# Mixing K and V of three of four batches by 64x64 matrices in four tiles of the array, with a new order of all units

## The chip, the cores and the metric

The kernel runs on one core of one Trainium2 chip. The metric is the device time of one execution in microseconds; a stated time is the median of several executions. Beside it stands one execution that was taken by the hardware profiler, from which all views below come. Its engines are named as the profile names them: PE multiplies matrices and PEld loads their weights, DVE and ACT do vector and activation work and empty PSUM, POOL is the fourth engine and also issues the casting loads, SP issues most other transfers.

## What is computed

```python
P = sort_net                                    # (4, 8, 8, 8): batch, head, 8x8
for _ in range(5):
    P = exp(P - max(P, -1)); P = P / sum(P, -1); P = P / sum(P, -2)
k_sorted = einsum('bhij,bhjcd->bhicd', P, k_b)  # blocks of 96 tokens, D = 64
v_sorted = einsum('bhij,bhjcd->bhicd', P, v_b)
attn = softmax(q_b @ k_sorted_b^T / sqrt(D))    # each block with itself
x = attn @ v_sorted_b                           # (4, 768, 512) over all heads
h = relu(x @ w_in)                              # 512 -> 1024, halves u and v
v_n = layernorm(v)                              # over 512 features
v_s = w_spatial @ v_n + b_spatial               # 768 x 768 over tokens
out = (u * v_s) @ w_out                         # 512 -> 512
```

There are 4 batches, 8 heads (4 pairs of heads), 768 tokens in 8 blocks of 96, and 64 features per head.

## The kernel before

The program is a list of units. The string `ORDER` names them one after the other, with their PSUM place, the engine that empties it, the batch and the head pair or tile; every engine runs what the units give it in that order, and nothing reorders it afterwards. `KT:1:A:2:0`, for example, mixes K of batch 2, head pair 0, into PSUM pair 1, and ACT empties it. PSUM is 8 banks; a place under 10 is a pair of banks, 10 to 17 a single bank.

The units and their lines: `L` loads a tensor over POOL's queue, casting to bf16, into one of eight slots (`ld`); `LH` brings half of batch 0's Q over SP's queue. `SK` is one round of the iteration on P. `MA`, `MB`, `MC` make masks and spreading matrices from the identity (L221 to L227), `PR` spreads P over the partitions by matmuls, and `P0` (on DVE, batch 0) and `PD` (on POOL, later batches) multiply it with a mask into `pd`: for each head a 128x128 matrix. A load puts 6 consecutive tokens of a head into each of 128 partitions, so a 128x128 matrix that is P[i,j] times an identity of 16 mixes the blocks without any movement of tokens.

`QT` turns Q by PE transposes, `QP` and `QX` by a copy and a transposing DMA (batches 2 and 3). `KT` mixes and turns K in one step: 12 matmuls with K as the weights (L395), the two heads of a pair in the two halves of the array's columns; `natural` copies the result to SBUF in token order. `VT` and `VB` do the same for V of batch 0 and turn it back. For batches 1 to 3 `VM` mixes V (L422: two matmuls of 128x128 weights and 384 columns per head pair) into the single buffer `vm`, and `VC` (L435) copies it by SP's DMAs, one per block, into `vb`, in which a block's 96 tokens lie in the partitions. `SC` computes a half of a head pair's scores (L454) and their exponent (L459); `AT` multiplies by `vb` (L500), and DVE divides by the sum (L507, L508).

Behind it comes the second part: `XT` or `XD` turn the attention's output, `VP` and `VH` compute the v half of the first layer (L567), `ST`, `LN` and `LA` its normalisation, `UP` the u half (L613), `SP` the spatial product (L625), `GT` the gating, `OP`, `OE` and `OS` the last layer and its output (L651). `SH`, `GH`, `OH`, `OI` and `OJ` do the last batch in smaller pieces. `WT` and `WW` turn the spatial weights.

Before the tail, `CK` gathers whether the sums of the softmax and of P left a safe range; `CF` (L747 to L749) adds it up into `flag`, `LF` (L752) loads it into a register of every engine, and `IF` branches to the tail or to a slower general path.

## Time and profile before

| | us |
|---|---|
| time, median of 3 runs (149.43 to 153.02) | 151.65 |
| span of the profiled execution | 147.7 |
| PE busy in it | 141.4 (96%) |
| PEld (weight loads, beside PE) | 101.0 (68%) |
| DVE busy | 115.1 (78%) |
| ACT busy | 85.2 (58%) |
| POOL busy | 39.1 (26%) |

The page gives no time of the profiled execution beside its span. Busy shares are averages over the whole span, in which different stages have different limits. The tables by windows of time tell the stages apart, and the chain of waits in order of time lists the work that each next piece waited for.

### The profile page before, as it was taken

Reading aid. Unit: us, or ns where it says so; the run is one execution under the profiler, and the core shown is the slowest. Engines: PE = TensorE matmul, PEld = TensorE weight load, DVE = VectorE, ACT = ScalarE, POOL = GpSimd, SP = SyncE. Lnnn points to the kernel's source line nnn. Section 1 sums busy time; section 2 is a strip of 40 time slices with the busy share of each in tenths; the row PEclk is TensorE's granted clock in tenths of the full one; section 3 lists DMA queues with packets and bytes.
Section 4 is the critical chain, followed back from the end, with each engine's and each line's share of the span. In section 5 each row is a group of like instructions: output and inputs, shape, how many; then the busy total and the mean of one; then the engine's idle time right before and its main releaser. Section 6 shows DMA issues by size and latency. Waiting matters only on the chain.

```text
span 147.7 us, 4114 instructions
## 1 busy us (share of the span) xinstructions
PE 141.4 (96%) x1691; PEld 101.0 (68%) x1691; DVE 115.1 (78%) x263; ACT 85.2 (58%) x125; POOL 39.1 (26%) x44
## 2 busy tenths in 40 slices
PE   6997999999999999999999999999999999999991
PEld 2466777857776667776877678768866876854760
DVE  3878899979987978867869879899558989846741
ACT  5357998988789447658793328756640046160040
POOL 6701994410000006991002640000002100004630
PEclk9999999999999999999999999999999999999999
DMA  2999999999999999899999999503602507007856
GB/s 60 278 204 205 204 207 201 208 225 243 227 233 231 204 200 269 131 177 211 206 202 175 213 239 278 132 0 83 28 0 60 190 2 284 0 2 266 307 210 228
DMA packets 37013, 25.93 MB, mean 176 GB/s; under 512 B 16704, under 2 KB 34112, under 8 KB 36992
## 3 DMA queue, kind: packets, MB, share of 16 engines
q0 software_dynamic: 14432, 12.19, 51.9%
q1 hardware_dynamic: 21552, 11.88, 33.8%
q10 hardware_dynamic: 1008, 1.57, 2.8%
q8 instruction: 14, 0.23, 0.6%
q14 instruction: 7, 0.06, 0.1%
HBM read 24.78 MB, written 6.29 MB: 210 GB/s over the span
## 4 chain that ended last, share of the span: by engine, by line
PE 82%; DMA 8%; DVE 5%; POOL 2%; issue 1%; ACT 1%; POOLq 0%; DVEq 0%
PE ps L625 16%; PE ps L567 15%; PE ps L613 14%; PE ps L651 11%; DMA k_in<-in_k_dram 8%; PE ps L681 5%; PE ps L500 4%; PE ps L395 4%; PE ps L701 4%; PE ps L454 4%; PE ps L422 3%; DVE x_sb L508 2%; PE ps L326 1%; PE ps L536 1%; PE ps L530 1%; DVE vb L124 1%
## 5 line engine op out<-in xcount | busy, mean ns | idle before, releaser
L642 POOL TENSOR_TENSOR gt<-z,u_sb 128x768 bf16<-128x768 f32 x7 | 11.4, 1642 | 68.0 <-DVE z L631 54.7
L459 ACT ACTIVATE ex_all<-ps 96x768 bf16<-96x768 f32 x32 | 23.7, 805 | 5.0 <-PE ps L454 4.1
L625 PE MATMUL ps<-wspT,v_sb 128*128 128x384 bf16 x144 | 25.0, 326 | 0.0
L567 PE MATMUL ps<-w_in_sb,xT 128*128 128x256 bf16 (+1 forms) x176 | 23.8, 283 | 0.0
L613 PE MATMUL ps<-xT,w_in_sb 128*128 128x384 bf16 x128 | 23.0, 326 | 0.0
L128 ACT ACTIVATE u_sb<-ps 128x768 bf16<-128x768 f32 x16 | 13.0, 811 | 17.3 <-PE ps L613 17.2
L508 DVE TENSOR_TENSOR x_sb<-ps,rec_all 96x512 bf16<-96x512 f32 x32 | 22.0, 687 | 1.1
L625 PEld LDWEIGHTS <-v_sb 128*128 128x128 bf16 x144 | 13.5, 98 | 8.4
L567 PEld LDWEIGHTS <-xT 128*128 128x128 bf16 x176 | 16.2, 98 | 4.0
L651 PE MATMUL ps<-w_out_sb,gt 128*128 128x256 bf16 x144 | 16.9, 273 | 0.0
L613 PEld LDWEIGHTS <-w_in_sb 128*128 128x128 bf16 x128 | 12.0, 98 | 7.0
L587 DVE BATCH_NORM_STATS2 stats<-v_sb 128x6 f32<-128x512 bf16 x24 | 16.2, 675 | 0.6 <-ACT v_sb L128 0.5
L122 ACT COPY o_sb<-ps 128x1024 f32<-128x1024 f32 (+2 forms) x11 | 8.9, 830 | 12.6 <-PE ps L701 9.3
L631 DVE TENSOR_TENSOR z<-ps,b_bc 128x768 f32<-128x768 f32 x12 | 11.5, 954 | 5.9 <-PE ps L625 5.1
L651 PEld LDWEIGHTS <-gt 128*128 128x128 bf16 x144 | 13.8, 98 | 2.0
L500 PEld LDWEIGHTS <-ex_all 96*128 96x128 bf16 x256 | 11.1, 97 | 2.6
L500 PE MATMUL ps<-vb,ex_all 96*128 96x65 bf16 x256 | 12.4, 193 | 0.1
L122 ACT CAST vm<-ps 128x768 bf16<-128x768 f32 x9 | 6.8, 807 | 9.7 <-PE ps L422 6.6
L694 POOL TENSOR_TENSOR gt<-z,u_sb 128x512 bf16<-128x512 f32 (+1 forms) x5 | 5.2, 1046 | 21.5 <-DVE z L687 21.5
L507 DVE RECIPROCAL rec_all<-ps 96x8 f32<-96x8 f32 x32 | 6.3, 196 | 5.5 <-PE ps L500 5.3
L130 DVE TENSOR_SCALAR v_sb<-ps 128x512 bf16<-128x512 f32 (+1 forms) x12 | 8.7, 727 | 1.7 <-PE ps L567 1.5
L236 PE MATMUL ps<-warm 128*128 128x512 bf16 (+3 forms) x38 | 8.5, 386 | 1.3 <-DVE warm L210 1.3
(100 smaller groups left out, 199.9 us busy)
## 6 DMA issues: line engine op xcount, KB each, us to landing
v_in<-in_v_dram POOLq DMA_DIRECT2D x4, 768.0 KB, 16.0
k_in<-in_k_dram POOLq DMA_DIRECT2D x4, 768.0 KB, 14.9
vb<-vm SPq DMA_DIRECT2D x24, 99.0 KB, 4.8
q_in<-in_q_dram POOLq DMA_DIRECT2D x3, 768.0 KB, 11.6
out_dram<-o_sb SPq DMA_DIRECT2D x9, 256.0 KB, 2.3
out_dram<-o_sb SPq DMA_DIRECT2D x4, 512.0 KB, 5.9
out_dram<-o_sb ACTq DMA_DIRECT2D x5, 256.0 KB, 2.3
ws_in<-in_moe_w_spatial_dram POOLq DMA_DIRECT2D x2, 576.0 KB, 18.9
```

The costliest lines, as they stand in the source:

```text
L122: nc.scalar.copy(out=out, in_=in_)
L128: nc.scalar.activation(out=out, in_=in_, func=AF.Relu)
L459: nc.scalar.activation(out=e_tile(b, hp, ih).rearrange("p h (x g) -> p h x g", g=G), in_=t[0:BLK, :, 0:HW].rearrange("p h (g x) -> p h x g ...
L500: nc.tensor.matmul(t[:, hh, ii * VW:ii * VW + D + 1], lhsT=e[:, c:c + 128], rhs=vb[b % 2][:, ih * NI + ii, 2 * hp + hh, 0:D + 1], start=Tr ...
L508: nc.vector.tensor_mul(out=x_sb[:, hp].rearrange("p i (h d) -> p h i d", h=2), in0=tv[:, :, :, 0:D], in1=_raw_ap(rec, 0, [rec.ap[0], [NI, ...
L567: nc.tensor.matmul(t[:, x, c:c + DH // parts], lhsT=st["xT", b][:, n // 3, kc, (n % 3) * 128:(n % 3 + 1) * 128], rhs=w_in_sb[:, kc, DH + c ...
L587: nc.vector.bn_stats(out=stats, in_=st["v_sb", b, n])
L613: nc.tensor.matmul(t[:, x, 0:HW], lhsT=w_in_sb[:, kc, mc * 128:(mc + 1) * 128], rhs=st["xT", b][:, ih, kc, :], start=(kc == 0), stop=(kc = ...
L625: nc.tensor.matmul(t[:, x, 0:HW], lhsT=st["v_sb", b, n][:, mc * 128:(mc + 1) * 128], rhs=wspT[:, 3 * x:3 * x + 3, n, :], start=(n == 0), s ...
L631: nc.vector.tensor_add(out=z.rearrange("p (x c) -> p x c", x=2), in0=t[:, :, 0:HW], in1=b_bc.rearrange("p (x c) -> p x c", x=2),)
L642: eng.tensor_mul(out=gt, in0=st["z", b, mc], in1=u)
L651: nc.tensor.matmul(t[:, x, c:c + w], lhsT=st["gt", b, mc][:, (n0 + x) * 128:(n0 + x + 1) * 128], rhs=w_out_sb[:, mc, c:c + w], start=(mc = ...
```

## The change

K and V of batches 1 to 3 are loaded with 12 consecutive tokens per partition and two heads of a pair in the two halves of the 128 partitions, 64 rows each (source runs of 3 KB, not 1.5). `pd` of these batches is one 64x64 matrix per head. `KP` takes the place of `KT` there: it mixes K of two head pairs by 48 matmuls of 64x64 weights and 64 columns, in turn for the four tiles of the array, into two PSUM pairs. `VM` mixes V by four matmuls of 64x64 weights and 384 columns in the four tiles. `VC` issues two DMAs per block, 48 partitions each. The heads of an odd pair change halves (`half`), so `QP` copies them in two pieces. Batch 0 keeps 128 rows (`mixed0`, `pd0`), with masks and spreading matrices of its own, so `MA`, `MB`, `MC` do each step twice and `PR` has 12 matmuls where it had 4.

The whole `ORDER` is new. K of batch 0 is loaded and mixed before V; V of batch 1 is loaded right behind; its mixing and that of batch 2 stand earlier; `CF` and `LF` stand side by side. Of each version the lines around the flag:

```
-UP:3:A:3:1:1 CF:11 VH:12:A:3:2 VH:13:A:3:1 OS:1:2:0:1 OS:1:2:1:2 LF VH:16:A:3:0 GT:D:2:2 OS:1:0:0:1:A OS:1:0:1:2:A
+OS:0:0:1:2:A OS:1:0:0:1:A OP:1:2:2:2 LA:3:4 LA:3:0 LA:3:1 OE:A:2:4 CF:11 LF SH:17:3:1:0 OE:D:2:2 OS:2:0 SH:16:3:2:0
```

The core of the rest of the diff; the same swap of halves is made in the Q transposes and in the general path:

```diff
@@ -169,7 +175,16 @@
 
 
     def u_L(what, *a):
-        if what in ("q", "k", "v"):
+        if what in ("k", "v") and int(a[0]) > 0:
+            b, lo, hi = (int(x) for x in a)
+            src = {"k": k, "v": v}[what]
+            if (what, b) not in st:
+                st[what, b] = ld_tile(f"{what}_in").rearrange("p h c -> p (h c)").rearrange("p (k c) -> p k c", k=HP)
+            nc.gpsimd.dma_start(
+                out=st[what, b][:, lo:hi],
+                in_=_raw_ap(src, (b * H + 2 * lo) * S * D, [[GR * D, 128], [2 * S * D, hi - lo], [1, GR * D]]),
+            )
+        elif what in ("q", "k", "v"):
             b, lo, hi = (int(x) for x in a)
             src = {"q": q, "k": k, "v": v}[what]
             if (what, b) not in st:
@@ -218,13 +233,16 @@
         make_identity(nc, ident)
 
     def u_MA():
-        nc.vector.reduce_sum(out=m32, in_=ident.rearrange("p (j t) -> p t j", t=TB), axis=AX.X)
+        nc.vector.reduce_sum(out=m32, in_=ident.rearrange("p (j t) -> p t j", t=TR), axis=AX.X)
+        nc.vector.reduce_sum(out=m16, in_=ident.rearrange("p (j t) -> p t j", t=TB), axis=AX.X)
 
     def u_MB():
-        nc.vector.tensor_copy(out=mask16, in_=m32)
+        nc.vector.tensor_copy(out=mask8, in_=m32)
+        nc.vector.tensor_copy(out=mask16, in_=m16)
 
     def u_MC():
-        nc.scalar.copy(out=spread, in_=ident[0:BH, 0:BH].to_broadcast([BH, BH, TB]))
+        nc.scalar.copy(out=spread, in_=ident[0:BH, 0:BH].to_broadcast([BH, BH, TR]))
+        nc.scalar.copy(out=spread16, in_=ident[0:BH, 0:BH].to_broadcast([BH, BH, TB]))
 
     def u_IV(n):
         t = vb[int(n)] if int(n) < 2 else vm
@@ -261,27 +279,38 @@
             nc.vector.transpose(out=p_t, in_=p16)
 
     def u_PR(ps):
-        pr = ps_tile(ps)[:, 0, 0:NB * BH].rearrange("p (i y) -> p i y", i=NB)
-        halves = pr.rearrange("p (k i) y -> p i k y", i=NI)
+        t = ps_tile(ps)[:, 0]
+        pr0 = t[:, 0:NB * H].rearrange("p (i y) -> p i y", i=NB)
+        halves = pr0.rearrange("p (k i) y -> p i k y", i=NI)
         for i in range(NI):
             nc.tensor.matmul(
-                halves[:, i], lhsT=spread[:, i * NB:(i + 1) * NB].rearrange("p j t -> p (j t)"),
-                rhs=p_t[:, 0:2 * BH].rearrange("p (k y) -> p k y", k=2), start=True, stop=True,
+                halves[:, i], lhsT=spread16[:, i * NB:(i + 1) * NB].rearrange("p j t -> p (j t)"),
+                rhs=p_t[:, 0:2 * BH].rearrange("p (k y) -> p k y", k=2)[:, :, 0:H], start=True, stop=True,
             )
-        st["pr"] = pr
+        pr = t[:, NB * H:NB * H + NB * (B - 1) * HP].rearrange("p (i y) -> p i y", i=NB)
+        parts = pr.rearrange("p (k i) y -> p i k y", i=NI)
+        turned_p = p_t.rearrange("p (k y h) -> p h k y", k=2, h=2)
+        for i in range(NI):
+            for hh in range(2):
+                nc.tensor.matmul(
+                    parts[hh * 64:hh * 64 + 64, i],
+                    lhsT=spread[:, i * NB:(i + 1) * NB].rearrange("p j t -> p (j t)"),
+                    rhs=turned_p[:, hh, :, HP:], start=True, stop=True,
+                )
+        st["pr0"], st["pr"] = pr0, pr
 
     def pd(b):
         if ("pd", b) not in st:
-            st["pd", b] = att.tile([128, H, 128], BF16, name="pd", tag="pd", bufs=2)
+            st["pd", b] = att.tile([128, HP, 64], BF16, name="pd", tag="pd", bufs=2)
         return st["pd", b]
 
     def u_P0(lo, hi):
         lo, hi = int(lo), int(hi)
-        n, pr = hi - lo, st["pr"]
+        n, pr = hi - lo, st["pr0"]
         nc.vector.tensor_mul(
-            out=pd(0)[:, lo:hi].rearrange("p h (i t) -> p h i t", t=TB),
+            out=pd0[:, lo:hi].rearrange("p h (i t) -> p h i t", t=TB),
             in0=_raw_ap(mask16, 0, [mask16.ap[0], [0, n], [0, NB], [1, TB]]),
-            in1=_raw_ap(pr, lo, [pr.ap[0], [1, n], [BH, NB], [0, TB]]),
+            in1=_raw_ap(pr, lo, [pr.ap[0], [1, n], [H, NB], [0, TB]]),
         )
 
     def u_PC(eng):
@@ -291,12 +320,14 @@
         b, lo, hi = int(b), int(lo), int(hi)
         n = hi - lo
         nc.gpsimd.tensor_mul(
-            out=pd(b)[:, lo:hi].rearrange("p h (i t) -> p h i t", t=TB),
-            in0=_raw_ap(mask16, 0, [mask16.ap[0], [0, n], [0, NB], [1, TB]]),
-            in1=_raw_ap(prep_sb, b * H + lo, [prep_sb.ap[0], [1, n], [BH, NB], [0, TB]]),
-        )
-
-
+            out=pd(b)[:, lo:hi].rearrange("p h (i t) -> p h i t", t=TR),
+            in0=_raw_ap(mask8, 0, [mask8.ap[0], [0, n], [0, NB], [1, TR]]),
+            in1=_raw_ap(prep_sb, (b - 1) * HP + lo, [prep_sb.ap[0], [1, n], [(B - 1) * HP, NB], [0, TR]]),
+        )
+
+    def half(b, hp, hh):
+        lo = 64 * (hh ^ (hp & 1) if b > 0 else hh)
+        return slice(lo, lo + 64)
 
     def turned(x, b, hp):
         if (x, b, hp) not in st:
@@ -309,11 +340,8 @@
         return st[x, b, hp]
 
     def natural(eng, dst, t):
-        to = dst[:, 0:S].rearrange("p (x g) -> p x g", g=G)
-        of = t[:, 0:S].rearrange("p (g x) -> p x g", g=G)
-        for n, e in enumerate(eng):
-            x = slice(n * 128 // len(eng), (n + 1) * 128 // len(eng))
-            copy(e, to[:, x], of[:, x])
+        to = dst[:, 0:S].rearrange("p (i b t g) -> p i b t g", i=NB, b=2, g=G)
+        copy(eng, to, t[:, :, 0:HW].rearrange("p b (g i t) -> p i b t g", g=G, i=NB))
 
     def q_tile(b):
         if ("qT", b) not in st:
@@ -372,10 +402,12 @@
         if ("qp", b) not in st:
             st["qp", b] = ld_tile("qp").rearrange("p h c -> p (h c)").rearrange(
                 "p (k g h d) -> p k g h d", k=HP, g=G, h=2)
-        copy(
-            eng, st["qp", b][:, hp].rearrange("p g h d -> p h g d"),
-            st["q", b][:, 2 * hp:2 * hp + 2].rearrange("p h (g d) -> p h g d", g=G),
-        )
+        to, of = st["qp", b][:, hp], st["q", b][:, 2 * hp:2 * hp + 2].rearrange("p h (g d) -> p h g d", g=G)
+        if hp % 2 == 0:
+            copy(eng, to.rearrange("p g h d -> p h g d"), of)
+        else:
+            for hh in range(2):
+                copy(eng, to[:, :, 1 - hh], of[:, hh])
 
     def u_QX(b, lo, hi):
         b, lo, hi = int(b), int(lo), int(hi)
@@ -388,22 +420,42 @@
         q_hp = q_tile(b)[rows, hp * S:(hp + 1) * S]
         return q_hp.rearrange("p (g t) -> p g t", g=G)[:, :, i * TB:(i + 1) * TB]
 
-    def mixed(x, name, ps, eng, b, hp):
+    def mixed(x, name, ps, eng, b, m):
+        ts = [ps_tile(n) for n in ps]
+        for n in range(GR):
+            for row in range(2):
+                g = (n + G * row) % GR
+                for o in range(2):
+                    rows = slice(64 * row, 64 * row + 64)
+                    nc.tensor.matmul(
+                        ts[o][half(b, o, row), g // G, (g % G) * 64:(g % G) * 64 + 64],
+                        lhsT=st[x, b][rows, 2 * m + o, g * D:(g + 1) * D], rhs=pd(b)[rows, 2 * m + o, :],
+                        start=True, stop=True,
+                    )
+        for o in range(2):
+            natural(eng[o], turned(name, b, 2 * m + o), ts[o])
+
+    def u_KP(ps0, ps1, eng, b, m):
+        mixed("k", "kT", (ps0, ps1), eng, int(b), int(m))
+
+    def mixed0(x, name, ps, eng, b, hp):
         t = ps_tile(ps).rearrange("p x c -> p (x c)")
         for g in range(G):
             for hh in range(2):
                 nc.tensor.matmul(
                     t[hh * 64:hh * 64 + 64, g * 128:(g + 1) * 128],
-                    lhsT=st[x, b][:, 2 * hp + hh, g * D:(g + 1) * D], rhs=pd(b)[:, 2 * hp + hh, :],
+                    lhsT=st[x, b][:, 2 * hp + hh, g * D:(g + 1) * D], rhs=pd0[:, 2 * hp + hh, :],
                     start=True, stop=True,
                 )
-        natural(eng, turned(name, b, hp), t)
+        copy(
+            eng, turned(name, b, hp)[:, 0:S].rearrange("p (x g) -> p x g", g=G),
+            t[:, 0:S].rearrange("p (g x) -> p x g", g=G))
 
     def u_KT(ps, eng, b, hp):
-        mixed("k", "kT", ps, eng, int(b), int(hp))
+        mixed0("k", "kT", ps, eng, int(b), int(hp))
 
     def u_VT(ps, eng, b, hp):
-        mixed("v", "vT", ps, eng, int(b), int(hp))
+        mixed0("v", "vT", ps, eng, int(b), int(hp))
 
     def u_VB(ps, eng, b, hp):
         b, hp = int(b), int(hp)
@@ -418,11 +470,13 @@
     def u_VM(ps, eng, b, hp):
         b, hp = int(b), int(hp)
         t = ps_tile(ps)
-        for hh in range(2):
-            nc.tensor.matmul(
-                t[:, hh, 0:G * D], lhsT=pd(b)[:, 2 * hp + hh, :], rhs=st["v", b][:, 2 * hp + hh, :],
-                start=True, stop=True,
-            )
+        for gh in range(2):
+            for hh in range(2):
+                rows = slice(64 * hh, 64 * hh + 64)
+                nc.tensor.matmul(
+                    t[64 * gh:64 * gh + 64, hh, 0:G * D], lhsT=pd(b)[rows, hp, :],
+                    rhs=st["v", b][rows, hp, gh * G * D:(gh + 1) * G * D], start=True, stop=True,
+                )
         copy(
             eng,
             vm[:, :, 2 * hp:2 * hp + 2, 0:D].rearrange("p g h d -> p h g d"),
@@ -432,10 +486,12 @@
     def u_VC(b, lo, hi, h0=0, h1=HP, eng="S"):
         b, heads = int(b), slice(2 * int(h0), 2 * int(h1))
         for i in range(int(lo), int(hi)):
-            queue(eng).dma_start(
-                out=vb[b % 2][:, i, heads].rearrange("c h d -> c (h d)"),
-                in_=vm[i * TB:(i + 1) * TB, :, heads].rearrange("t g h d -> t g (h d)"),
-            )
+            for gh in range(2):
+                rows = slice(64 * gh + i * TR, 64 * gh + (i + 1) * TR)
+                queue(eng).dma_start(
+                    out=vb[b % 2][gh * TR * G:(gh + 1) * TR * G, i, heads].rearrange("c h d -> c (h d)"),
+                    in_=vm[rows, :, heads].rearrange("t g h d -> t g (h d)"),
+                )
 
     def e_tile(b, hp, ih):
         e = ex[count["e"] % NE]
@@ -450,7 +506,7 @@
         for ii in range(NI):
             i = ih * NI + ii
             for hh in range(2):
-                rows = slice(hh * 64, hh * 64 + 64)
+                rows = half(b, hp, hh)
                 nc.tensor.matmul(
                     t[:, hh, 0:HW].rearrange("p (g x) -> p g x", g=G)[:, :, ii * TB:(ii + 1) * TB],
                     lhsT=kT[rows, i * BLK:i * BLK + 128], rhs=q_runs(b, hp, rows, i),
```

How the change moves instructions is shown at three places. First, PE around the flag. Before, from the last matmuls ahead of `CF` (L747) to `LF` (L752):

```order
L613 MATMUL ps<-xT,w_in_sb 128x384
L747 LDWEIGHTS ones
L747 MATMUL ps<-bad,ones 1x5 [waits DVE_49]
L567 LDWEIGHTS xT [waits DMAHW5_49]
L567 MATMUL ps<-w_in_sb,xT 128x256 [waits DVE_49]
...
L567 LDWEIGHTS xT
L752 TENSOR_LOAD flag [waits DVE_49]
L567 MATMUL ps<-w_in_sb,xT 128x256 [waits Activation_49]
```

Now:

```order
L707 MATMUL ps<-w_out_sb,gt 128x256
L803 LDWEIGHTS ones
L803 MATMUL ps<-bad,ones 1x5 [waits Activation_49]
L737 LDWEIGHTS v_sb [waits DVE_49]
L808 TENSOR_LOAD flag [waits DVE_49]
L737 MATMUL ps<-wspT,v_sb 128x512
L737 LDWEIGHTS v_sb [waits DVE_49]
```

The load stood behind 16 matmuls of `VH` that follow the flag's own matmul; now only one weight load lies between them.

Second, DVE where it empties batch 2's mixed V into `vm` for the first time. Before (L631 adds the bias to the spatial product, L642 is the gating):

```order
L631 TENSOR_TENSOR z<-ps,b_bc 128x768 [waits PE_49]
L642 TENSOR_TENSOR gt<-z,u_sb 128x768
L631 TENSOR_TENSOR z<-ps,b_bc 128x768 [waits DVE_49,PE_49]
L124 CAST vm<-ps 128x2x6x64 [waits DMAHW4_49,DMAHW3_49,DMAHW5_49,DMAHW2_49,DMAHW6_49,DMAHW1_49,DMAHW7_49,DMAHW0_49,PE_49]
L587 BN_STATS stats<-v_sb 128x6 [waits Activation_49]
L588 BN_AGGR mv<-stats 128x2 [waits DVE_49]
L124 CAST kt_all<-ps 128x768 [waits PE_49] x2
L130 TENSOR_SCALAR v_sb<-ps 128x512 [waits PE_49,Activation_49]
```

Now:

```order
L644 BN_AGGR mv<-stats 128x2 [waits DVE_49]
L563 RECIPROCAL rec_all<-ps 96x8 [waits PE_49]
L564 TENSOR_TENSOR x_sb<-ps,rec_all 96x2x4x64 [waits DVE_49]
L132 TENSOR_SCALAR v_sb<-ps 128x512 [waits PE_49,Activation_49]
L126 CAST vm<-ps 128x2x6x64 [waits DMAHW4_49,DMAHW3_49,DMAHW5_49,DMAHW2_49,DMAHW6_49,DMAHW1_49,DMAHW7_49,DMAHW0_49,PE_49]
L643 BN_STATS stats<-v_sb 128x6
L644 BN_AGGR mv<-stats 128x2 [waits DVE_49]
L563 RECIPROCAL rec_all<-ps 96x8 [waits PE_49]
L564 TENSOR_TENSOR x_sb<-ps,rec_all 96x2x4x64 [waits DVE_49]
```

In both, the copy waits for all eight queues on which the copies from `vm` of batch 1 were sent; before it lies behind the first spatial products, now among the first layer's v half (L132) and the normalisation (L643, L644) of batch 0 and the attention of batch 1.

Third, SP's queue at the end of the copies of batch 1's V into `vb` (L435 before, L491 now). Before:

```order
L435 DMA vb_98<-vm 96x1x528 [waits DMAHW0_49]
L435 DMA vb_98<-vm 96x1x528 [waits DMAHW1_49]
L518 DMA_TRANSPOSE xT<-x_sb 128x16x96 [waits DMAHW2_49,DVE_49]
L382 DMA_TRANSPOSE qT<-qp 128x24x128 [waits DMAHW3_49,PE_49,Activation_49]
L518 DMA_TRANSPOSE xT<-x_sb 128x16x96 [waits DMAHW4_49,DVE_49]
L435 DMA vb_97<-vm 96x1x528 [waits DMAHW5_49,DVE_49,Activation_49]
```

Now:

```order
L491 DMA vb_102<-vm 48x1x528 [waits DMAHW0_49]
L491 DMA vb_102<-vm 48x1x528 [waits DMAHW1_49]
L491 DMA vb_101<-vm 48x1x528 [waits DMAHW2_49,DVE_49,Activation_49]
L491 DMA vb_101<-vm 48x1x528 [waits DMAHW3_49]
L491 DMA vb_101<-vm 48x1x528 [waits DMAHW4_49,PE_49]
```

Before, the eight copies are followed by the transposing DMAs of batch 1's output and batch 2's Q (L518, L382); now sixteen copies stand there, half as many partitions each, and batch 2's copies, which wait for DVE and ACT to have filled `vm` again, follow them directly.

More of the change, by code (lines that the diff above doesn't have):

```diff
@@ L88 @@
     TB = 128 // NB
+    GR = 2 * G
+    TR = 64 // NB
     BH = B * H
@@ L134 @@
     p_t = const.tile([BH, NB * NB], BF16, name="p_t")
-    spread = const.tile([BH, BH, TB], BF16, name="spread")
+    spread = const.tile([BH, BH, TR], BF16, name="spread")
+    spread16 = const.tile([BH, BH, TB], BF16, name="spread16")
     rowsum = const.tile([BH, NB], FP32, name="rowsum")
@@ L471, in u_SM @@
             for hh in range(2):
-                rows = slice(hh * 64, hh * 64 + 64)
+                rows = half(b, hp, hh)
                 nc.tensor.matmul(
```

115 lines of the change are left out of this document (64 added, 51 removed).

## The prediction

> **What bounds the kernel now.** I read the page first: how long the span is and which engine fills it.
>
> ```profile
> span 147.7 us, 4114 instructions
> PE 141.4 (96%) x1691; PEld 101.0 (68%) x1691; DVE 115.1 (78%) x263; ACT 85.2 (58%) x125; POOL 39.1 (26%) x44
> PE 82%; DMA 8%; DVE 5%; POOL 2%; issue 1%; ACT 1%; POOLq 0%; DVEq 0%
> ```
>
> PE is busy 96% of the span and holds 82% of the chain that ended last. An average does not say where, so the second view is the windows of 4 us (busy us of each engine in each).
>
> ```profile
> 12.00:16.00 4.00, 3.36 (x84) 2.78 (x83) 3.42 (x7) 3.14 (x5) 1.91 (x2) 1.00 1.32 206
> 16.00:20.00 4.00, 3.88 (x103) 3.18 (x98) 3.85 (x6) 3.91 (x7) 4.00 (x6) 1.00 1.31 202
> 20.00:24.00 4.00, 3.79 (x95) 3.12 (x94) 3.90 (x10) 3.58 (x6) 2.72 (x4) 1.00 1.32 205
> 24.00:28.00 4.00, 3.86 (x74) 2.92 (x72) 3.82 (x9) 4.00 (x6) 0.89 (x1) 1.00 1.30 208
> 28.00:32.00 4.00, 4.00 (x103) 3.17 (x98) 3.10 (x6) 3.58 (x6) 1.99 (x2) 1.00 1.18 210
> 140.00:144.00 4.00, 4.00 (x29) 2.45 (x28) 1.96 (x5) 1.76 (x3) 1.41 (x2) 1.00 0.51 197
> ```
>
> The columns are PE, PEld, DVE, ACT, POOL and the granted clock. From 28 us to the tail PE is full at clock 1.00. Before that DVE is as full as PE: 14.99 of the 16 us from 12 to 28. So there are two stages: up to 28 us a vector instruction that is added costs time, and after that only PE work and a wait that PE itself meets cost time.
>
> The third view is the chain of waits in order of time, whose rows say what PE work costs when nothing holds it up.
>
> ```profile
> 27.68 0.79 PE ps L395 x24
> 41.24 0.28 PE ps L454 x8
> 41.52 1.41 PE ps L613 x8
> 52.85 0.65 PE ps L422 x4
> 56.98 1.46 PE ps L395 x48
> 59.84 0.87 PE ps L567 x8
> 60.72 0.62 PE ps L454 x24
> 61.34 0.98 PE ps L567 x8
> 62.31 1.30 PE ps L613 x8
> ```
>
> **The stream of PE, part by part.** An N=384 matmul of the full array in V mixing (L422) takes 0.65/4 = 162.5 ns, an N=256 one (L567) 0.87/8 = 109 ns: 0.42 ns per column and 1 to 2 ns besides. By that a lone N=128 matmul takes 55 ns, N=96 42 ns, N=64 29 ns. K mixing now (L395, 128 rows by 64 columns of the array, N=128) takes 1.46 us for 48, which is 28 ns each once 0.1 us for the change of shape (below) is taken off: two at a time, one in each half of the columns. SC (L454, 64 rows by 128 columns, N=96) takes (0.62 - 0.1)/24 = 22 ns each: two at a time in the halves of the rows.
>
> *K.* The three later batches have 144 such matmuls, 144 x 28 ns = 4.0 us. The change has 288 with N=64, 29 ns alone, and four at a time they give 288/4 x 29 = 2.1 us: 1.9 us less. No row shows four tiles at once. Pairs along columns and pairs along rows are both shown, so I take four; the bounds are four at a time (2.1 us) and two (4.2 us), with a third possibility among the rivals.
>
> *V.* 24 x 162.5 ns = 3.9 us become 48 in four tiles, 48/4 x 162.5 = 1.95 us: 1.95 us less. The bounds are 1.95 and 3.9.
>
> *Changes of tile shape.* The same eight L567 matmuls take 0.87 us behind matmuls of their own shape and 0.98 behind SC; the eight of L613 take 1.30 and 1.41. A change of shape costs 0.1 us. Counted along PE's instruction order, before has 55 such changes and the new order 72, since KP, VM and SC now alternate with full-array work: 17 x 0.095 = +1.6 us. The Trainium skill ("TensorEngine Tiling (Array Packing)", Key Properties) says that a change of tiling mode, unlike a change of tile, drains the engine; it gives no price. The rows above agree with a drain and price it at 0.1 us.
>
> Net of the stream: -1.9 - 1.95 + 1.6 = **-2.3 us**. From 28 us on PE is full, so this falls straight on the end.
>
> **The early stage.** Up to 28 us the price is DVE's. I lined up the two orders where PE has done the same work (about 22.5 us of it: before up to the third Q transposition of batch 1, after up to the second KP of batch 1) and compared DVE's list.
>
> ```profile
> 11.39 0.12 DVE L224 CAST mask<-m 128x16 bf16<-128x16 f32 x1
> 11.90 0.75 DVE L281 TENSOR_TENSOR pd<-mask,ps 128x256 bf16<-128x256 bf16 x2 [0.38 <-ACT qT L122]
> L221 DVE TENSOR_REDUCE m<-ident 128x16 f32<-128x128 bf16 x1 | 0.4, 363 | 0.0
> L124 DVE COPY qT<-ps 128x768 bf16<-128x768 bf16 x4 | 2.0, 546 | 0.0
> L124 DVE COPY xT<-ps 128x768 bf16<-128x768 bf16 x2 | 1.1, 544 | 0.0
> L124 DVE CAST vm<-ps 128x768 bf16<-128x768 f32 x3 | 2.8, 947 | 0.0
> ```
>
> DVE has one more V evacuation (0.95), two more Q copies (2 x 0.55), one fewer xT copy (-0.54), a second mask reduction (0.36) and a second mask cast (0.12): +1.99 us. It idled 16 - 14.99 = 1.01 us from 12 to 28, which the new order can fill. That leaves 1.0 us late. The bounds are 2.0 (nothing filled) and -1.0: the added work lies in gaps and K, which now lands ahead of V, lets PE recover its own idle from 12 to 28 (0.64 + 0.12 + 0.21 + 0.14 = 1.1 us by the windows).
>
> Next to it lies the copy of mixed V of batch 1 into blocks, DMAs on SP's queue, 16 now where 8 were.
>
> ```profile
> 27.67 5.21 SPq L435 DMA_DIRECT2D vb<-vm  x8
> DMA to landing us min/median/max: 5.7/7.3/8.8
> DMA to landing us min/median/max: 2.8/4.8/8.8
> ```
>
> The first landing row is of those eight, the second of all 24. The issue takes 5.21/8 = 0.65 us each, so 16 take 10.4 us. V of batch 1 is evacuated earlier, so I estimate the first issue at 23 us by the place in the order, the last at 33.4. What is late next: vm has one buffer, and the first evacuation of batch 2's V into it, on DVE and then ACT, waits for all of these copies; in the new order it stands at about 35.5 us, and behind it on DVE stand the normalisation and the attention evacuations. PE would feel it about 1 us later, at 36.4, at the next V mixing that wants its PSUM pair. In before, batch 2's V is mixed only at 52.85, and no such wait could arise. Landing 2.8 us after the last issue (36.2) costs nothing, 4.8 (38.2) costs 1.8, 7.3 (40.7) costs 4.3. The stretch has full DMA queues in both kernels, but the pieces are half as large, so I take something short of the middle row. This wait and DVE's lateness lie over each other and do not add: together **+1.5 us**, bounds -1.0 and 4.3.
>
> **The flag.** The range check puts a flag through PE, DVE and a register load on every engine.
>
> ```profile
> 119.38 0.17 PE L747 MATMUL ps<-bad,ones 128*1 128x5 bf16 x1
> 119.92 0.14 DVE L748 TENSOR_REDUCE ends<-ps 1x1 f32<-1x5 f32 x1
> 120.09 0.14 DVE L749 CAST flag<-ends 1x1 int32<-1x1 f32 x1
> L752 PEldq TENSOR_LOAD <-flag x1: 493/493/493, 120.3 to 120.3; - x1
> 119.54 2.73 PE ps L567 x24
> ```
>
> From the L747 matmul to the end of the load on PE's queue it is 120.27 + 0.49 - 119.38 = 1.4 us. Before, 16 matmuls of L567 stand between the two on PE, and the row at 119.54 shows PE never stopping. In the new order the load stands straight behind the L747 matmul, with one weight load between. PE works only for the 0.17 of that matmul and stands for 1.4 - 0.17 = **+1.2 us**; bounds 0 (the load does not hold matmuls back) and 1.4.
>
> **Costed at nothing.** PD on POOL has a quarter of the elements, and POOL is busy 26%. The split Q copies for odd head pairs go to ACT and DVE after 28 us; ACT has 42% of the span free. The eight further P-spreading matmuls are N=12 and lie in PE's early idle; without that cover they cost about 0.2 us. SP's queue has 24 more DMAs, 24 x 0.65 = 16 us over the span; past batch 1 the V copies of batches 2 and 3 have over 10 us before their attention begins. If that cover were gone, each batch would lose its own 5.2 us.
>
> **The sum**, on the profiled span: 147.7 - 2.3 + 1.5 + 1.2 = 148.1 us, +0.4. The page gives no time of the profiled execution beside its span; the median of the runs shown is 151.65, 3.95 us above the span, for what lies around it and for the difference of one run from another. I take that as unchanged and move the median: 151.65 + 0.4 = 152.05, **152.0 us**. The runs shown spread from 149.43 to 153.02, so 2%, 3.03 us, is about what a measurement of this kernel can tell from no change: below 148.6 is faster, above 154.7 slower.
>
> **The rivals.**
>
> *Everything is hidden (faster).* The stream saves its 2.3 us, the early idle of PE is recovered (-1.0), and the flag's wait is covered: 151.65 - 3.3 = 148.35 us. For it: K now comes ahead of V, and K's landing is the longest piece of the early chain:
>
> ```profile
> 3.90 11.51 DMA k_in<-in_k_dram
> ```
>
> Against it: DVE has 2 us more to do there with 1 us of gaps, and one weight load is little cover for the flag.
>
> *Two tiles at a time (slower).* If a 64x64 tile shares the array only with the tile beside it, KP takes 4.2 us in all and VM 3.9: the stream saves nothing, and the changes of shape stay. 151.65 + 1.6 + 1.5 + 1.2 = 155.95 us. For it: no row shows more than two at once. Against it: both directions of pairing are in the trace. It decides from the point where four tiles give under a third of what I put down.
>
> *Batch 1's V copies land late (slower).* At the landing times of the eight of batch 1, 7.3 to 8.8 us, PE waits 4.3 to 5.8 us at batch 2's V mixing: 151.65 - 2.3 + 5.05 + 1.2 = 155.6 us. It decides when the last copy lands later than about 40.5 us. For it: the loads fill the queues then. Against it: the pieces are half as large, and over the whole program the middle landing is 4.8 us.
>
> *A floor per matmul (slower).* If every small matmul cost what L395 shows each, whatever its N and its tiles, KP would take 288 x 28 ns = 8.1 us and not 2.1: 152.0 + 6.0 = 158.0 us. Against it stands SC with its 22 ns. The Trainium skill ("TensorE: Matmul & The Clock Gate", Wait — 56ns, not 53.3ns?) states such a floor, about 25 ns from start to start however small N is; by it KP would take an estimated 288 x 25 ns = 7.2 us. SC's 22 ns are already under it, so the trace does not bear it out between tiles.
>
> **How the numbers follow.** Forecast 0.36, everything hidden 0.23, two at a time 0.16, V copies late 0.16, the floor 0.03, two of the slower cases together 0.06. The forecast's own range, from its two early bounds in the middle and the flag's, is 150 to 153.5, so nearly all of it is within 2%; everything hidden gives 0.19 faster and 0.04 same; two at a time 0.14 slower and 0.02 same; the late copies 0.12 slower and 0.04 same; the rest is slower; 0.01 of the forecast lies on the faster side and 0.02 on the slower. Faster 0.20, same 0.43, slower 0.37. The range has to reach into the cases of both signs: below to 148.0, a little past the hidden case, above to 156.4, past two at a time and the middle of the late copies; what is left out is the far end of both, about 0.2.
>
> **What would show it.** In the changed profile: KP's 48 matmuls in 48/4 x 29 = 0.35 us and 0.1 us for the change of shape, VM's four in 0.16 + 0.1; V mixing of batch 2 following without a hole after 35 us, or a hole there ended by a DMA; a hole of about 1.2 us on PE behind the flag's matmul; PE reaching its unbroken stretch about 1 us later than 28 us. The prediction is wrong if KP takes 0.7 us or more each, if the hole at batch 2's V exceeds 4 us, or if full-array matmuls behind 64x64 tiles pay well over 0.1 us.

## The result and the profile after

The changed kernel takes 163.0 us in the median of four runs (162.39 to 165.02), the kernel before 150.67 us beside it: a ratio of 1.085 (95% interval 1.076 to 1.095), 8.5% slower. The forecast was 152.0 us in a range of 148.0 to 156.4. The ratios here and below leave out executions more than 1.5% above the fastest of their kernel, and the profile is of such a one, the run of 165.02 us, with a mean granted clock of 0.941 where the other three had 0.966 to 0.976, so that some 2 us of the losses below belong to it alone.

The page of the changed kernel first: span, busy times, granted clock in 40 slices, and the chain that ended last.

```profile
span 163.2 us, 4502 instructions
PE 146.7 (90%) x1864; PEld 102.4 (63%) x1867; DVE 118.8 (73%) x272; ACT 84.1 (52%) x124; POOL 34.9 (21%) x43
PEclk9997599975896999999999999999999999999997
PE 69%; DMA 11%; DVE 8%; SPq 3%; ACT 3%; issue 2%; DVEq 0%; ACTq 0%
```

PE's busy time grew, though it has less to do, because the clock fell to half three times (slices 4 to 5, 9 to 11 and 13 of 40) before the drop at the very end. In the chain, DMA and SP's queue have entered. The windows of the changed kernel (the columns as above) show where, and three wide windows of each kernel how much.

```profile
12.00:16.00 4.00, 2.72 (x74) 2.35 (x74) 3.12 (x6) 2.02 (x4) 3.32 (x7) 0.80 1.28 209
16.00:20.00 4.00, 4.00 (x56) 2.98 (x54) 2.72 (x4) 2.14 (x3) 2.76 (x4) 0.50 1.20 205
28.00:32.00 4.00, 3.39 (x121) 2.63 (x121) 3.93 (x9) 3.01 (x5) 0.00 (x0) 1.00 1.17 219
32.00:36.00 4.00, 2.84 (x85) 2.32 (x86) 2.35 (x6) 3.15 (x5) 0.36 (x2) 0.86 1.19 224
36.00:40.00 4.00, 3.19 (x21) 1.86 (x21) 1.33 (x3) 1.81 (x3) 1.69 (x4) 0.50 1.17 228
44.00:48.00 4.00, 1.33 (x15) 0.44 (x9) 0.76 (x2) 0.00 (x0) 0.00 (x0) 1.00 1.21 214
48.00:52.00 4.00, 3.07 (x26) 2.24 (x25) 2.65 (x6) 2.70 (x4) 0.00 (x0) 0.57 1.18 234
52.00:56.00 4.00, 4.00 (x59) 2.78 (x57) 3.62 (x8) 3.34 (x5) 0.00 (x0) 1.00 0.75 169
...
0.00:28.00 28.00, 24.15 (x359) 16.40 (x362) 20.67 (x64) 18.44 (x29) 13.04 (x25) 0.88 1.11 197
28.00:52.00 24.00, 17.82 (x305) 11.70 (x306) 13.54 (x28) 12.66 (x18) 2.05 (x4) 0.79 1.19 224
52.00:157.90 105.90, 104.69 (x1207) 74.26 (x1204) 84.31 (x181) 52.91 (x78) 19.82 (x14) 1.00 0.57 135
```

The same three of the kernel before:

```profile
0.00:28.00 28.00, 25.01 (x416) 17.29 (x418) 22.52 (x69) 20.81 (x32) 14.94 (x24) 1.00 1.16 196
28.00:52.00 24.00, 24.00 (x334) 16.93 (x329) 20.84 (x47) 18.65 (x28) 1.99 (x2) 1.00 1.23 225
52.00:144.40 92.40, 92.40 (x951) 66.76 (x948) 71.45 (x148) 45.68 (x66) 22.16 (x18) 1.00 0.73 155
```

To compare them I give each matmul of the two traces a price close to the prediction's (0.417 ns per column and 2.5 ns, divided by the tiles side by side, and 0.095 us for each change of shape). The sum is 136.8 us before and 133.9 now: 2.9 us less. Of this 0.65 us is no saving: three matmuls of 512 columns have no record in the trace now. What PE's time holds beyond the sum is lost to waits and half clock:

| lost on PE, us | before | changed | sixteen copies alone | eight copies, new order | and batch 1's K in 128 rows |
|---|---|---|---|---|---|
| to 28 us | 6.6 | 9.6 | 6.8 | 8.6 | 8.6 |
| 28 to 52 us | 0.3 | 11.8 | 4.2 | 6.3 | 2.7 |
| from 52 us to PE's end | 0.7 | 2.7 | 11.4 | 2.6 | 4.7 |

Changed against before that is 3.0 + 11.5 + 2.0 - 2.9 = 13.6 us, which is, but for rounding, PE's end at 157.9 against 144.4. (The last three columns are of experiments below; the missing records add 0.2 us to the first row and 0.4 to the second of the changed kernel and of the two with eight copies.)

The chain of waits in order of time tells what fills 28 to 52 us; behind it the SP queue's row for the sixteen copies, and PE's three longest waits past the start.

```profile
30.59 7.41 DMA vb<-vm
38.01 9.59 DMA vb<-vm
...
48.08 0.81 ACT vm L124
...
48.93 0.54 PE ps L476 x4
...
64.96 0.51 PE ps L430 x48
...
70.09 0.45 PE ps L476 x8
```

```profile
L491 SPq DMA_DIRECT2D vb<-vm x16: 681/681/902, 25.3 to 38.0; - x16
```

```profile
PE ps L476 <- ACT vm L124: 3.4, 1, 3.4
PE ps L510 <- issue: 1.4, 1, 1.4
...
PE ps L737 <- DVE flag L805: 0.9, 1, 0.9
```

The eighth copy is issued at 30.59 us. From the tenth on each waits until the copy eight places ahead of it has landed, so the sixteenth goes out at 38.01 (at the first ones' pace of 0.73 us it would have been 36.4) and lands 9.59 us later, at 47.60. By the semaphore events of the trace the first copy lands at 31.0 and the sixteenth at 47.6: 1.1 us from one landing to the next. The eight copies of twice the size in the kernel before land from 33.3 to 41.1 us, also 1.1 us apart; in this stretch it is the number of copies that counts, not their size. Only behind the last landing does ACT, which has waited 4.7 us by then, empty batch 2's mixed V, and PE, out of other work by 45.5, goes on at 48.93.

### The profile page after: what moved, and what is told of

The parts are those of the page before. It is cut to its first block, busy times and chain, and to the rows that moved or that the text cites. A ratio compares the mean times of both kernels' runs of the same rounds, so it can differ in the third digit from the quotient of the medians.

```text
span 163.2 us, 4502 instructions
## 1 busy us (share of the span) xinstructions
PE 146.7 (90%) x1864; PEld 102.4 (63%) x1867; DVE 118.8 (73%) x272; ACT 84.1 (52%) x124; POOL 34.9 (21%) x43
## 4 chain that ended last, share of the span: by engine, by line
PE 69%; DMA 11%; DVE 8%; SPq 3%; ACT 3%; issue 2%; DVEq 0%; ACTq 0%
PE ps L681 15%; PE ps L669 12%; DMA vb<-vm 10%; PE ps L623 10%; PE ps L707 10%; PE ps L737 5%; PE ps L510 4%; PE ps L556 3%; PE ps L757 3%; SPq L491 3%; PE ps L445 2%; ACT kt_all L124 1%; PE ps L430 1%; PE ps L465 1%; DVE vm L126 1%
## 5 line engine op out<-in xcount | busy, mean ns | idle before, releaser
L698 POOL TENSOR_TENSOR gt<-z,u_sb 128x768 bf16<-128x768 f32 x8 | 13.6, 1714 | 72.0 <-DVE z L687 72.0
L623 PE MATMUL ps<-w_in_sb,xT 128*128 128x256 bf16 (+1 forms) x174 | 25.6, 299 | 0.6 <-issue 0.4
L623 PEld LDWEIGHTS <-xT 128*128 128x128 bf16 x176 | 17.0, 102 | 5.4 <-issue 2.4
L130 ACT ACTIVATE v_sb<-ps 128x512 bf16<-128x512 f32 (+1 forms) x12 | 7.6, 633 | 19.5 <-PE ps L623 19.4
L687 DVE TENSOR_TENSOR z<-ps,b_bc 128x768 f32<-128x768 f32 x12 | 11.5, 956 | 8.3 <-PE ps L681 8.3
L707 PE MATMUL ps<-w_out_sb,gt 128*128 128x256 bf16 x144 | 17.1, 273 | 0.0
L643 DVE BATCH_NORM_STATS2 stats<-v_sb 128x6 f32<-128x512 bf16 x24 | 16.2, 673 | 1.1 <-ACT v_sb L130 1.0
L669 PEld LDWEIGHTS <-w_in_sb 128*128 128x128 bf16 x128 | 11.8, 98 | 7.0
L556 PEld LDWEIGHTS <-ex_all 96*128 96x128 bf16 x256 | 11.5, 99 | 4.2 <-issue 1.1
L556 PE MATMUL ps<-vb,ex_all 96*128 96x65 bf16 x256 | 13.0, 196 | 0.8 <-DMA vb<-vm 0.6
L124 ACT CAST kt_all<-ps 128x768 bf16<-128x768 f32 x9 | 7.0, 803 | 10.0 <-PE ps L430 8.9
L130 ACT ACTIVATE u_sb<-ps 128x768 bf16<-128x768 f32 x12 | 9.7, 811 | 4.0 <-PE ps L669 4.0
L510 PE MATMUL ps<-qT,kt_all 64*128 64x96 bf16 x256 | 9.8, 217 | 2.1 <-issue 1.4
L510 PEld LDWEIGHTS <-kt_all 64*128 64x128 bf16 x256 | 6.7, 100 | 6.0 <-issue 4.3
```

Source lines behind the costliest of these rows:

```text
L124: nc.scalar.copy(out=out, in_=in_)
L130: nc.scalar.activation(out=out, in_=in_, func=AF.Relu)
L510: nc.tensor.matmul(t[:, hh, 0:HW].rearrange("p (g x) -> p g x", g=G)[:, :, ii * TB:(ii + 1) * TB], lhsT=kT[rows, i * BLK:i * BLK + 128], r ...
L556: nc.tensor.matmul(t[:, hh, ii * VW:ii * VW + D + 1], lhsT=e[:, c:c + 128], rhs=vb[b % 2][:, ih * NI + ii, 2 * hp + hh, 0:D + 1], start=Tr ...
L623: nc.tensor.matmul(t[:, x, c:c + DH // parts], lhsT=st["xT", b][:, n // 3, kc, (n % 3) * 128:(n % 3 + 1) * 128], rhs=w_in_sb[:, kc, DH + c ...
L643: nc.vector.bn_stats(out=stats, in_=st["v_sb", b, n])
```

## The experiments

Each kernel was timed against the kernel before on the same chip in three rounds. The ratios and their intervals are of these pairs.

**The structure in the old order, and sixteen copies alone.** The first kernel is the changed one with the old list of units (`KT:2:D:1:1 KT:1:A:1:2` and the two `KT` ahead of it become `KP:0:2:AD:1:0 KP:0:1:AA:1:1`, and so on). The second is the kernel before with this edit:

```diff
-            queue(eng).dma_start(
-                out=vb[b % 2][:, i, heads].rearrange("c h d -> c (h d)"),
-                in_=vm[i * TB:(i + 1) * TB, :, heads].rearrange("t g h d -> t g (h d)"),
-            )
+            for x in range(2):
+                queue(eng).dma_start(
+                    out=vb[b % 2][48 * x:48 * x + 48, i, heads].rearrange("c h d -> c (h d)"),
+                    in_=vm[i * TB + 8 * x:i * TB + 8 * x + 8, :, heads].rearrange("t g h d -> t g (h d)"),
+                )
```

> The whole change of structure (64x64 matrices in four tiles for K and V of batches 1 to 3, sixteen V copies per batch, two-piece Q copies) in the order of units of the kernel before; where two K mixings of a pair of head pairs stood apart, the joint one stands at the later place. Theory A (the new order puts batch 2's V mixing and batch 1's attention in front of V copies that are not there yet, and the clock falls in the holes): the copies have until 52 us here, so no hole over 1 us, clock 1.00 from 28 us on, and the stream's saving shows: 146 to 150 us. Rival B (the structure itself is what costs: sixteen copies, changes of tile shape, denser PE instructions): over 154 us in any order.

> The kernel before, with each V copy of batches 1 to 3 sent as two DMAs of 48 partitions, so sixteen per batch; nothing else. Theory A: issue and landing stretch to about 12 us + 9 us from 27.7 us, so the last lands near 49 us; batch 2's V mixing at 52 us is not held, but the attention of the second half of batch 1, which ran at 43 to 47 us, waits up to 5 us: 151 to 156 us. Rival B (sixteen copies cost by themselves wherever they stand): 156 us or more. If the copies don't matter: 150.7 within 2%.

Measured: 165.68 us (ratio 1.101, 1.088 to 1.114) and 165.49 us (1.099, 1.088 to 1.110). Both expectations of theory A fail, and rival B has both times: with sixteen copies the time is 165 us or more in the old order too, and with nothing else changed. Of the second kernel, what PE waited for, and SP's row for batch 2's copies:

```profile
PE ps L501 <- DMA vb<-vm: 9.6, 6, 4.2
```

```profile
L436 SPq DMA_DIRECT2D vb<-vm x16: 681/681/1359, 61.6 to 73.6; - x16
```

Here it is the attention itself that waits, in all three batches (2.0, 5.4 and 2.2 us), not batch 2's V mixing. Half a copy takes 0.68 us of SP's queue where a whole one took 0.60, and sixteen take 12 us from the first issue to the last where eight took under 5. Behind the waits the clock stands at half for 10.2 us.

**V back in 128 rows, and warm-up matmuls.** The first is the changed kernel with V mixing and V copies as before. The second adds `DM:13:3:512` ahead of `PR:10` and behind it.

> The changed kernel with V of batches 1 to 3 back in 128 rows: two full-array matmuls per V mixing, eight V copies per batch, the mask products for V on POOL beside those for K; K stays in four tiles and the order stays. Theory A: the last of eight copies lands at about 38 to 40 us instead of 47.6, the 3.4 us hole at batch 2's V mixing goes, and with it one or two of the three stretches at half clock; V's saving of 1.95 us is given back: 154 to 158 us. If the number of copies is not what matters: 163 + 2 = 165 us.

> The changed kernel with six more warm-up matmuls (512 columns, 0.22 us each), three in front of the spreading of P and three behind it, where PE stands idle 0.8 us each time. Theory C (the clock's fall at 14.4 us comes of PE's idle between 10.5 and 13 us and costs the early stage its lateness): clock 1.00 to 28 us, 2 to 4 us less, 159 to 161 us. If idle there is not what the clock goes by: the same half clock from 14 to 21 us and 163 us, or a little more.

Measured: 157.25 us (1.044, 1.033 to 1.054), as theory A has it; and 164.25 us (1.086, 1.073 to 1.099), which misses theory C's 159 to 161. The six matmuls do keep the clock at 1.00 to 34 us, and nothing is gained: the last copy now lands at 47.07, half a microsecond earlier, and the same hole follows.

```profile
PE ps L476 <- ACT vm L124: 3.6, 1, 3.6
PE ps L510 <- issue: 1.7, 1, 1.7
```

What the early half clock costs was hidden behind the copies. Of the second kernel's windows, one early and one behind the copies' wait:

```profile
20.00:24.00 4.00, 3.77 (x81) 2.62 (x76) 3.59 (x7) 3.94 (x7) 0.92 (x2) 1.00 1.26 208
36.00:40.00 4.00, 3.45 (x22) 1.69 (x20) 0.89 (x2) 1.43 (x3) 1.22 (x2) 0.50 1.17 226
```

**Four tiles with eight copies.** If the columns of a 64x64 matrix are ordered by token first and block second, the 16 rows of a block in `vm` lie 8 partitions apart over all 128, and one DMA takes them:

```diff
-            out=pd(b)[:, lo:hi].rearrange("p h (i t) -> p h i t", t=TR),
+            out=pd(b)[:, lo:hi].rearrange("p h (t i) -> p h i t", t=TR),
...
-        copy(eng, to, t[:, :, 0:HW].rearrange("p b (g i t) -> p i b t g", g=G, i=NB))
+        copy(eng, to, t[:, :, 0:HW].rearrange("p b (g t i) -> p i b t g", g=G, i=NB))
...
+            queue(eng).dma_start(
+                out=vb[b % 2][:, i, heads].rearrange("c h d -> c (h d)"),
+                in_=vm.rearrange("(t i) g h d -> i t g h d", i=NB)[i][:, :, heads].rearrange("t g h d -> t g (h d)"),
+            )
```

It ran in the new order, in the old order, and (third) as K alone in four tiles in the old order; the fourth is the first with `LF` two spatial products later (`CF:11 SH:17:3:1:0 ... SH:16:3:2:0 GH:P:3:2:0 LF`).

> The changed kernel with the columns of the 64x64 matrices in another order (token of eight first, block second), so that a block's rows in vm lie eight partitions apart over all 128 and one DMA per block takes all 96 tokens: eight V copies per batch and not sixteen, with both mixings still in four tiles and the order as it is. Theory A (the sixteen copies are what costs): the last copy of batch 1 lands at 38 to 40 us, the hole at batch 2's V mixing goes, and the time falls to 152 to 157 us, below that of the kernel with V in 128 rows (157.25). Rival (something else in the structure or the order): over 160 us.

> The same with eight copies, in the order of units of the kernel before. Theory A: against the same structure with sixteen copies in this order (165.7 us) the waits of the attention for the copies go (5.9 us on PE and the half clock that follows them), and what is left is the stream's saving of 2.3 us against a later joint K mixing: 148 to 153 us. If the four tiles or the changes of shape cost as such: 155 us or more.

> K of batches 1 to 3 in four tiles, V as in the kernel before (128 rows, eight copies), in the order of units of the kernel before. Theory A: K's saving of 1.9 us, less some 10 more changes of shape (1 us) and the later joint mixing (up to 2 us): 150 to 153 us, within 2% of before. If the four tiles cost as such, 155 us or more.

> The first of these (eight copies, new order) with the load of the flag two spatial products later, so that 12 matmuls of 512 columns (2.6 us) stand on PE between the flag's matmul and the load. By the profile of the changed kernel PE stood 0.9 us there: 0.9 us less than the first of these, no hole behind the flag's matmul. If the load's wait is hidden anyway: the same time within 0.3 us.

Measured: 156.98 us (1.042, 1.030 to 1.053), 160.33 us (1.064, 1.048 to 1.080), 160.07 us (1.064, 1.048 to 1.080) and 155.75 us (1.040, 1.026 to 1.053). The first is the cleanest test of the sixteen copies, since nothing but their number and the order of columns differs: 6 us. Its row on SP's queue, how long the copies took to land, and when ACT empties batch 2's mixed V:

```profile
L489 SPq DMA_DIRECT2D vb<-vm x8: 580/597/661, 24.2 to 28.8; - x8
DMA to landing us min/median/max: 5.5/8.0/9.1
L124 ACT CAST vm<-ps x3: 798/801/820, 42.5 to 44.8; 128x768 bf16<-128x768 f32 x3
```

The eight land about as late after their issue as in the kernel before (5.7 to 8.8), only the last issue is 9.2 us earlier than that of sixteen, and the last landing, at 37.9, comes 4.6 us before ACT wants `vm`. The fourth saves 1.2 us more, of which 0.9 is the hole behind the flag; it is gone. The second and third miss: K in four tiles needs two PSUM pairs at once, and in the old order both were still being emptied (PE waits 2.2 us for that in the second, and 2.3 us more for batch 2's V copies). The second kernel's windows show PE thinly filled from 24 us on, with two stretches of half clock:

```profile
24.00:28.00 4.00, 3.46 (x53) 2.41 (x49) 3.63 (x8) 3.03 (x5) 0.75 (x1) 0.67 1.29 206
28.00:32.00 4.00, 2.49 (x123) 2.23 (x121) 1.85 (x3) 2.71 (x5) 1.51 (x2) 0.90 1.18 209
32.00:36.00 4.00, 3.55 (x72) 3.15 (x67) 2.23 (x4) 2.08 (x4) 0.00 (x0) 0.57 1.18 241
```

**PE's instructions.** What remained in the new order was a wait of PE near 31 us that nothing in the profile releases ("issue" above). The trace has a queue of instruction packets of 16 KB, 14 before and 16 now, whose number fits PE's instructions:

```profile
q8 instruction: 16, 0.26, 0.6%
```

In the changed kernel these start at 15.55, 22.28, 30.70 and 36.67 us, and PE, which ran 242 matmuls and weight loads from 28 to 32 us, stands from 31.6 to 33.0. The place of the wait bears it out. Eight of the 14 traces have it, 0.2 to 1.9 us long, and in all eight it stands behind the 956th or 957th matmul or weight load, whatever unit that belongs to. In no trace does PE pass this place earlier than 1.2 us after the third of the packets has ended; in the kernel before it gets there 1.4 us after that end and does not wait. To test it, K's matmuls of the kernel before were split, with nothing else changed:

```diff
-            for hh in range(2):
-                nc.tensor.matmul(
+            for c in ((0, 128),) if b == 0 else ((0, 64), (64, 128)):
+                for hh in range(2):
+                    nc.tensor.matmul(
```

and, the other way round, batch 1's K was put back into 128 rows (`KT:1:D:1:0 KT:2:A:1:1` for `KP:1:2:DA:1:0`, and the same for the other two head pairs; POOL gets two more mask products of 1.2 us), in the new order and in the old:

> The kernel before, with each matmul of K mixing of batches 1 to 3 split into two of 64 columns: the same array work (two halves of the columns at a time) but 288 matmuls and 288 weight loads where 144 were, which is the instruction count of the changed kernel's K mixing. Theory D (PE runs out of instructions: 16 KB of them, 256, come by one DMA packet about every 6 us while the loads fill the DMA engines, and 96 more between 24 and 32 us are too many): a stall of 1 to 2 us on PE near 30 us with no releaser, with or without a stretch of half clock behind it, 152 to 156 us. Rival (the stall that the changed kernel shows at 31.6 us has another cause): within 1% of before.

> The kernel of eight V copies, new order and later flag load (155.75 us), with K of batch 1 mixed in 128 rows by twelve matmuls per head pair again, which takes 48 matmuls and 48 weight loads out of PE's stream near 30 us. Theory D: the stall of 1.7 us with no releaser at 30.8 us goes, and the stretch at half clock behind it: 150 to 153 us. Rival: the stall stays, 155 to 157 us.

> The same structure (batch 1's K in 128 rows, K of batches 2 and 3 and V of all three in four tiles, eight V copies) in the order of units of the kernel before. The joint K mixing of batch 1, at which the same order lost about 8 us between 24 and 36 us with its waits and the half clock, is gone. If those waits were the price: 147 to 151 us. If the four tiles cost something wherever they stand: 154 us or more.

Measured: 154.82 us (1.020, 1.009 to 1.030), 156.05 us (1.039, 1.030 to 1.049) and 157.83 us (1.051, 1.038 to 1.063). The first has the wait that the kernel before has not, and something dearer behind it:

```profile
PE ps L501 <- DMA vb<-vm: 3.2, 1, 3.2
...
PE ps L326 <- issue: 0.9, 1, 0.9
```

The count of instructions makes the wait: theory D holds for it. What the wait costs is less certain. The interval reaches from 0.9% to 3.0%, and the profile is of the longest of the four runs, 157.39 us (the others took 152.27, 153.88 and 155.75). In this run batch 2's copies go out a microsecond later (first at 58.7, not 57.6 us), and the attention of batch 2, which in this order follows its copies closely, waits 3.2 us at 65 to 68 us and then works at half clock; no trace shows whether the shorter runs do the same. The second misses the 150 to 153 us of theory D: in its profile the wait is down to 0.2 us and the half clock behind it is gone, and the time is still the same (155.75 with the wait), since the gain met a new wait.

```profile
PE ps L442 <- DVE z L697: 2.2, 1, 2.2
```

The sums behind the first spatial products wait for the bias, which landed 28.6 us after its issue. The third was expected at 147 to 151 us if the joint mixing was the price. Its clock stands at 1.00 and PE loses only 0.4 us from 28 to 52 us, but 8.4 behind, of which 2.7 are the attention of batch 2 waiting for its copies.

**The bias earlier.** `BI` moved from behind the loads of Q and K of batch 2 to ahead of them.

> The kernel with eight V copies, new order, later flag load and batch 1's K in 128 rows (156.05 us), with the load of the spatial bias issued ahead of the third Q and K loads on POOL's queue instead of behind them. In the profile of that kernel the first spatial products' sums waited for the bias, which landed 28.6 us after its issue, and PE stood 2.2 us behind them at 57.65 us. If that is a place where the stall taken away upstream came back: the hole goes and the time falls by 2 us, to 153 to 154.5 us, still above the kernel before. If the loads that now come later take its place: within 0.7 us of 156.

Measured: 155.15 us (1.033, 1.023 to 1.042), 0.9 us less, between the two expectations, with intervals that overlap: the wait for the bias is gone, and the K load that it now precedes takes 0.8 us of its place.

```profile
PE ps L442 <- DMA k_in<-in_k_dram: 0.8, 1, 0.8
```

No version of the four tiles beat the kernel before.

## Why the prediction was wrong, point by point

*The stream of PE: right in its mechanism, a little too good in size.* 48 matmuls of K in four tiles take (0.51 - 0.1)/12 = 34 ns for four, where 29 was used; four of V (0.45 - 0.1)/2 = 175 ns for 162.5. With these K saves 4.0 - 2.4 = 1.6 us and V 3.9 - 2.1 = 1.8, and with 1.6 for the changes of shape the stream is 1.8 us shorter, not 2.3. (The 2.9 of the sums above is not a measurement of this: it uses the prediction's price for four tiles and lacks three records.) Four tiles do run side by side, and the rivals of two tiles and of a floor per matmul are out.

*The copies of batch 1's V: the step that failed.* The term took a first issue at 23 us, sixteen issues at 0.65 us each, ending at 33.4 us, and under 4.8 us for the landing: PE at most 1.8 us late. Measured: first issue 25.3, 0.73 us from one issue to the next, the later ones held until an earlier copy has landed (1.6 us in all), last issue 38.0, landing 9.6 us, so 47.6 us. Most of the error is the landing: it was taken as shorter because the pieces are half as large, but landings come 1.1 us apart for either size, so sixteen take twice as long as eight. A second error hid part of the first: ACT wanted `vm` at about 43.4 us (42.5 with eight copies), not at 35.5, so a landing some 10 us late left a hole of 3.4. The rival that named this place had it decided by a last landing after 40.5 us, and so it was, but priced it at 5 us. The edit's price was 6 us between the kernels of sixteen and eight copies in the new order and 14 us alone in the old. The prediction counted the eight queues on which the evacuation waits, but not that the later copies wait for them too.

*Copies of batches 2 and 3: right at nothing.* "Over 10 us before their attention begins" held in the new order (PE waited for none of them). It does not hold in the old, in which eight copies just fit: with sixteen alone 7.6 of the 9.6 us of waits are theirs.

*The clock: not in the sum at all.* It was taken as 1.00 from the profile before. In the changed kernel it was at half for 17.1 us to 52 us, in three stretches of 6.8, 6.8 and 3.4; the higher mean clock of the other three runs means, as an estimate, some 8 to 11 us less of it. I take it as an amplifier and not as a first cause: kept at 1.00 early, it gained nothing. No run kept it at 1.00 in the two later stretches with the sixteen copies in place, so their price apart from the copies is not shown.

*The early stage: the number within reach, the mechanism not.* +1.0 was forecast, 3.0 measured to 28 us, with 6.8 us of half clock in it; with eight copies, and the clock at 1.00 there, it is 2.0, the upper bound. That it meets the bound is luck: DVE, whose added work was to be the price, is busy for 13.33 of the 16 us from 12 to 28 there, less than the 14.99 before.

```profile
12.00:28.00 16.00, 12.98 (x305) 10.12 (x305) 13.33 (x25) 12.42 (x18) 7.95 (x12) 1.00 1.23 208
PE ps L445 <- DVE pd L310: 0.8, 1, 0.8
PE ps L476 <- DMA v_in<-in_v_dram: 0.7, 1, 0.7
```

PE waited among others for the first mask products and for the landing of V, which now comes behind K. The prediction let this lateness and that of the copies lie over each other, +1.5 together; measured, they add.

*Instructions: not seen.* KP doubles PE's instructions at its densest place: 0.9 to 1.9 us of waiting in six profiles (0.2 and 0.4 in two more), and a half clock behind it in the five that have KP there.

*The flag: right.* 0.9 us for 1.2.

What stays open: the changed kernel is 12 us slower; 6 are shown to be the copies and about 1 the flag. The last kernel, without either, is still 5 us slower than the one before. With eight copies and batch 1's K in 128 rows PE loses 2.0 us more than before to 28 us, 2.4 from 28 to 52 and 4.0 behind, in many small waits for ACT, DVE and DMA besides the bias; no run took them apart. No run has the old structure in the new order either, so what the order costs by itself is not shown.

## What to carry to other kernels

A cheaper matrix operation that needs its data in another layout is paid in the transfers which restore that layout: count those DMAs, their issue, how far apart they land, and how many may be in flight, before the matmuls. Where one engine is full at 96%, everything around it is just in time, and a wait taken away at one place (1.5 us near 31 us) came back at the next (2.2 us at 55.7 us); a sum of terms then needs the slack of each follower beside it. A kernel that runs at full clock shows nothing of what the clock does once work thins out.

## What the runs showed of the hardware

The clock fell without an idle step. It changed in steps of 3.41 us, and in the changed kernel it fell at 34.8 us after a step in which PE's longest wait was 1.4 us and its matmuls were busy just over half of the time (1.86 of 3.41 us). The Trainium skill (TensorE: Matmul & The Clock Gate, What's actually happening) has the throttle come back after at least one idle window of some 3.4 us; the step agrees with these traces, the need for idleness does not. As an estimate from all 14 profiles: take the columns streamed in a step, weighted by the part of the array's rows and columns in use, as a share of what full clock allows (3.41 us at 0.417 ns per column). The 24 steps that half clock followed lie at 0.36 or less (0.35 and 0.29 ahead of the first two falls of the changed kernel); the other steps, nearly 600, lie at 0.37 or more. If that is the measure, packing small matmuls into tiles does not raise it, and the time saved lowers it.

PE's instructions come by DMA beside the loads, about 240 to a packet (3382 matmuls and weight loads in 14 packets before); with the loads on the DMA engines, two packets lay 6 to 8 us apart between 15 and 37 us (before and changed), which a stage of small matmuls outruns. A DMA of 48 partitions holds SP's queue longer (0.68 us) than one of 96 (0.60).
